# One queue for the stores of gated tiles: SyncE instead of ScalarE, and later in program order

## The chip, the cores and the metric

The kernel runs on one core of a Trainium2 chip. The metric is the device time of one execution in microseconds (us); lower is better. The core has five engines with a queue each: TensorE (PE in the profile, with its weight loads as PEld), VectorE (DVE), ScalarE (ACT), GpSimd (POOL) and SyncE (SP). An engine works through its queue in order. A DMA is begun by an instruction in the queue of SyncE, ScalarE or GpSimd.

## What is computed

The reference mixes two maps of one input `x` (2048 rows, 640 columns) by a gate of each row. Part A is the real part of a Fourier transform over columns and rows, done with matrices. Part B picks, for each row and each of 32 heads, two of 256 experts by product keys, and sums their weighted outputs.

```python
g = sigmoid((x * gate_w).sum(-1, keepdims=True))
# A: y = Cr @ (x @ Dr^T) - Ci @ (x @ Di^T)
a = einsum("bsd,ed->bse", x, dft_hid_re);  b = einsum("bsd,ed->bse", x, dft_hid_im)
y = einsum("ts,bse->bte", dft_seq_re, a) - einsum("ts,bse->bte", dft_seq_im, b)
# B: two best of 16 keys in each half, two best of the four sums, gates, experts
s1 = einsum("nhd,ed->nhe", q1, k1);  s2 = einsum("nhd,ed->nhe", q2, k2)
...
act = gelu(einsum("nd,nhkd->nhk", xf, u[top_e]))
out = einsum("nhk,nhk,nhkd->nd", softmax(top_s), act, v[top_e])
return g * y + (1 - g) * out
```

## The kernel before, in words

**The sequence product.** The kernel turns part A round: it first multiplies the sequence matrices (real and imaginary, 2048 x 2048) with `x`, and later the result with the 640 x 640 hidden matrices. The sequence product runs over 8 columns `q`: two matrices `w` times four blocks `c` of 512 rows (`q = 4 w + c`). Each column is summed over 16 pieces `s` of 128 rows of `x`, so there are 128 pieces `n` in all, `n = 16 q + s`. In one piece, `seq_piece(n)`, TensorE adds to five banks, one for each `d` of five 128-wide parts of the 640 columns. For float32 accuracy each product is three matmuls of high and low parts (`mm3`, L146, L147, L148): high x high, high x low and low x high.

**How a piece is fed.** `load_piece(n + 5)` has SyncE begin the load of a 128 x 512 block of the matrix (`wf<-in_wsre` or `wf<-in_wsim`, L180). `split_piece(n + 3)` makes its high and low parts in one of four slots of `WS`. In most pieces ScalarE rounds the high part (L141) and GpSimd subtracts it (L142). In others, among them the even pieces from 76 to 90, ScalarE makes the high part (L191) and its negative (L192), and GpSimd begins a DMA that adds the block from memory once more onto the negative (L194). The parts `X[s]` of `x` are on the chip only in part: eleven of 16 are stored in `xd` and loaded again by SyncE (L473, `get_x`), in the first half of the product three pieces or more before they are used.

**The gated tiles.** In the last piece of a column ScalarE copies the five banks to five staging tiles `ST` (L249). A row of gates is loaded, VectorE multiplies the five tiles with it (`gate_piece`, L220), and `store_piece` stores them to `pd[w, c]` (L230). Seven columns are stored by ScalarE, the last one by SyncE. The staging tiles come round again in the next column, 16 pieces later. Column 5 stays on the chip too, as `P22`, and is changed in place by later sums (`sum_parts`, L1062).

**The order.** The program is written out in one order, with a table `then`: `at(n, f)` puts a step behind piece `n`, and `follow(n)` runs the steps of piece `n` in the order in which they were put there. Every engine gets its instructions in that order. Between the products of a piece, `run_bg` takes steps of background work from a queue: the picking of experts, and later the building of expert masks (`experts`, L869 on VectorE), which TensorE uses in groups of 128 small matmuls (L883) whose results ScalarE scales (L820) and VectorE adds up (L826). SyncE also does transposing DMAs for the expert rows (L719), and the loads of `draw` (L921), which become the hidden matrices `DD` (split at L141 and L142).

Of the kernel before, what the change touches and what calls it, by code (L numbers as in the profile page):

```python
# [28 lines left out]
NC = S // TC  # L29
NPC = 2 * NC * NT  # L30
KD = D // P
# [78 lines left out]
def gated_mix_kernel(ctx: ExitStack, tc: tile.TileContext, xT, xn, dreT, dimT, wsre, wsim, wq, kT, uT, vv, gw, out):  # L110
    nc = tc.nc
# [38 lines left out]
    pd = {(w, c): dram.tile([KD, P, TC], F32, name=f"pd{w}{c}", tag=f"pd{w}{c}") for w in range(2) for c in range(NC)}  # L150
# [48 lines left out]
    def at(n, f, *args):  # L199
        then.setdefault(n, []).append(lambda: f(*args))  # L200
# [8 lines left out]
    grow, staged, P22 = {}, {}, {}  # L209
# [5 lines left out]
    def gate_piece(q):  # L215
        g = grow.pop(q)
        w, c = divmod(q, NC)
        for d in range(KD):
            f = staged.pop((q, d))
            nc.vector.scalar_tensor_tensor(f, f, -1.0 if w else 1.0, g, op0=OP.mult, op1=OP.mult)  # L220
            bg.credit -= 0.75
            staged[q, d] = f

    def store_piece(q, chunks=range(KD)):
        w, c = divmod(q, NC)
        if q == NC + 1:
            P22.update((d, staged[q, d]) for d in range(KD))
        eng = nc.sync if q == 2 * NC - 1 else nc.scalar
        for d in chunks:
            eng.dma_start(pd[w, c][d], staged.pop((q, d)))  # L230

    def seq_piece(n):
        w, c, s = pieces[n]
# [18 lines left out]
    for q in range(2 * NC):  # L252
        n = NT * (q + 1)
        at(n + (2 if q == 0 else -2 if q > 1 else -1), load_row, q)
        at(n + (7 if q == 0 else 0), gate_piece, q)
        if q in (1, 2, 3, 4):
            for d in range(KD):
                at(n + 1 + d, store_piece, q, (d,))
        else:
            at(n + (12 if q == 0 else 1), store_piece, q)  # L260


    p1_stack = ctx.enter_context(ExitStack())
# [63 lines left out]
    for n in range(WARM):  # L327
        c = slice(0, 2 * P) if n < WARM - 1 else slice(2 * P, TC)
# [172 lines left out]
    n = b + 2  # L501
# [274 lines left out]
    for p in range(NP):  # L776
        n = N0 + 4 * p + min((p + 1) // 2, 3)
# [296 lines left out]
    for k, (n, m) in enumerate(((-1, 2), (0, 4), (5, 7), (7, 9), (10, 12))):  # L1074
        n, m = NT * (NC + 2) + n, NT * (NC + 2) + m
# [255 lines left out]
```

## Time and profile before

| | |
|---|---|
| median of 3 runs | 753.0 us (752.62 to 753.67) |
| the profiled execution's own time | 753.65 us |
| its span, first to last instruction | 751.9 us |
| mean granted TensorE clock | 0.997 |
| busy: TensorE, VectorE, ScalarE, GpSimd | 745.9, 579.0, 337.0, 344.0 us |
| DMA | 171.17 MB, mean 228 GB/s |
| stores `pd<-ST` begun by ScalarE / by SyncE | 35 / 5, of 256 KB each |

The profile is of one execution. A row of a timeline gives the start, the duration, the engine (with q for its queue alone, where it issues or waits), the source line, the operation, and in brackets the idle time ahead of it and what ended that. A row of waits gives the total, the number and the longest. The chain of waits is followed back from the end: at each step to what released the instruction, or to the one before it on its engine. The duration of a DMA in the chain is from its start to its landing.

### The profile page before, as it was taken

The numbers are of one execution on the slowest core, as the hardware profiler recorded it, in microseconds if no ns is written. First come the engines' busy times: TensorE is split into PE (matmuls) and PEld (weight loads), VectorE is DVE, ScalarE is ACT, GpSimd is POOL, SyncE is SP. The second block draws the span as 40 slices with busy tenths as digits, with TensorE's granted clock in tenths as the row PEclk, the third lists the DMA queues.
The fourth block names the chain that finished last, engine by engine and source line by source line (L and its number), as shares of the span: only waits on it lengthen the run. The fifth ranks groups of instructions, "written<-read, shape, count | busy, mean of one in ns | idle before, by whom it ended". The sixth has DMA issues, their size and how long they took to land.

```text
span 751.9 us, 12032 instructions
## 1 busy us (share of the span) xinstructions
PE 745.9 (99%) x4437; PEld 606.4 (81%) x4437; DVE 579.0 (77%) x721; ACT 337.0 (45%) x564; POOL 344.0 (46%) x286
## 2 busy tenths in 40 slices
PE   9999999999999999999999999999999999999998
PEld 7777777888888888888888887888888888888887
DVE  6864087595999899999999959998798874357651
ACT  4335234543545745655454565422344553443451
POOL 5533324540532424235145655544356693487253
PEclk9999999999999999999999999999999999999999
DMA  9999999887656785971498675398855789875302
GB/s 338 372 384 359 331 364 380 232 237 234 140 171 148 195 245 134 254 204 54 134 406 276 150 189 160 95 320 265 285 194 185 227 259 305 258 235 178 112 29 71
DMA packets 84491, 171.17 MB, mean 228 GB/s; under 512 B 16080, under 2 KB 21328, under 8 KB 84176
## 3 DMA queue, kind: packets, MB, share of 16 engines
q1 hardware_dynamic: 70960, 146.13, 57.9%
q0 software_dynamic: 5472, 9.96, 8.4%
q10 hardware_dynamic: 8000, 14.31, 5.2%
q8 instruction: 35, 0.57, 0.3%
q14 instruction: 24, 0.20, 0.1%
HBM read 136.40 MB, written 32.39 MB: 224 GB/s over the span
## 4 chain that ended last, share of the span: by engine, by line
PE 96%; DMA 2%; SPq 1%; ACT 0%; POOL 0%; issue 0%; DVE 0%; ACTq 0%
PE b L146 30%; PE b L147 30%; PE b L148 30%; PE b L383 2%; PE b L242 2%; PE b L883 1%; DMA wf<-in_wsim 1%; DMA WS<-in_wsim 1%; PE b L329 1%; SPq L719 0%; ACT rows L724 0%; POOL DD L142 0%; SPq L921 0%; SPq L180 0%; ACT DD L141 0%
## 5 line engine op out<-in xcount | busy, mean ns | idle before, releaser
L146 PE MATMUL b<-WS,X 128*128 128x512 f32 x620 | 243.8, 393 | 0.0
L147 PE MATMUL b<-WS,X 128*128 128x512 f32 x620 | 241.9, 390 | 1.9 <-DMA WS<-in_wsim 1.9
L148 PE MATMUL b<-WS,X 128*128 128x512 f32 x620 | 241.8, 390 | 0.0
L142 POOL TENSOR_TENSOR WS<-wf,WS 128x512 fp32r<-128x512 f32 x89 | 131.5, 1481 | 177.4 <-ACT WS L141 173.1
L146 PEld LDWEIGHTS b<-WS,X 128*128 128x128 f32 x620 | 116.7, 188 | 28.2 <-issue 4.1
L147 PEld LDWEIGHTS b<-WS,X 128*128 128x128 f32 x620 | 116.8, 188 | 26.0 <-DMA WS<-in_wsim 2.3
L148 PEld LDWEIGHTS b<-WS,X 128*128 128x128 f32 x620 | 116.7, 188 | 24.6
L141 ACT ACTIVATE WS<-wf 128x512 fp32r<-128x512 f32 x89 | 55.5, 627 | 110.5 <-PE b L148 68.3
L869 DVE TENSOR_TENSOR hot<-rows,wtab 128x1024 f16<-128x1024 f16 x56 | 54.1, 1000 | 12.4 <-PE b L883 12.4
L142 POOL TENSOR_TENSOR xl<-xf,xh 128x640 fp32r<-128x640 f32 x16 | 26.8, 1680 | 72.5 <-ACT xh L141 72.5
L570 ACT ACTIVATE sc<-b 128x512 f32<-128x512 f32 x32 | 19.9, 620 | 78.8 <-PE b L148 75.0
L194 POOL DMA_DIRECT2D WS<-in_wsre x30 | 26.3, 878 | 61.0 <-ACT WS L192 59.7
L142 POOL TENSOR_TENSOR WS<-ra,WS 128x512 fp32r<-128x512 f32 x33 | 46.6, 1423 | 15.3 <-ACT WS L141 10.4
L141 ACT ACTIVATE WS<-ra 128x512 fp32r<-128x512 f32 x47 | 29.4, 631 | 42.7 <-PE b L148 30.6
L625 DVE TENSOR_TENSOR eq<-sc,mm 128x1024 f16<-128x1024 f32 x32 | 44.4, 1388 | 0.9
L632 DVE TENSOR_REDUCE tied<-eq 128x64 f32<-128x1024 f16 x32 | 39.0, 1218 | 0.9
L623 DVE TENSOR_REDUCE mm<-sc 128x64 f32<-128x1024 f32 x32 | 38.7, 1210 | 0.2
L220 DVE SCALAR_TENSOR_TENSOR ST<-ST,grow 128x512 f32<-128x512 f32 x40 | 33.9, 902 | 0.6 <-ACT ST L249 0.6
L142 POOL TENSOR_TENSOR WP<-ra,WP 128x512 fp32r<-128x512 f32 x13 | 19.3, 1492 | 31.0 <-ACT WP L141 30.9
L147 PE MATMUL b<-WU,xh 128*128 128x512 f32 x80 | 31.1, 389 | 0.0
L146 PE MATMUL b<-WU,xh 128*128 128x512 f32 x80 | 31.1, 389 | 0.0
L148 PE MATMUL b<-WU,xl 128*128 128x512 f32 x80 | 31.1, 389 | 0.0
(213 smaller groups left out, 1431.0 us busy)
## 6 DMA issues: line engine op xcount, KB each, us to landing
X<-xd SPq DMA_DIRECT2D x36, 640.0 KB, 6.5
wq<-in_wq SPq DMA_DIRECT2D x32, 640.0 KB, 7.5
wf<-in_wsim SPq DMA_DIRECT2D x64, 256.0 KB, 4.9
wf<-in_wsre SPq DMA_DIRECT2D x63, 256.0 KB, 6.6
ra<-pd SPq DMA_DIRECT2D x40, 256.0 KB, 3.4
pd<-ST ACTq DMA_DIRECT2D x35, 256.0 KB, 4.5
WS<-in_wsre POOLq DMA_DIRECT2D x30, 256.0 KB, 6.2
xd<-X SPq DMA_DIRECT2D x11, 640.0 KB, 9.1
```

Of the source, the lines that this page charges most:

```text
L141: nc.scalar.activation(h, f, AF.Copy)
L142: eng.tensor_sub(l, f, h.bitcast(F32))
L146: nc.tensor.matmul(o, wh, ah, start=first, stop=False, skip_group_check=more)
L147: nc.tensor.matmul(o, wh, al, start=False, stop=False, skip_group_check=more)
L148: nc.tensor.matmul(o, wl, ah, start=False, stop=last, skip_group_check=more)
L194: nc.gpsimd.dma_start(l, (wsre, wsim)[w][c, s], accum_op=OP.add)
L220: nc.vector.scalar_tensor_tensor(f, f, -1.0 if w else 1.0, g, op0=OP.mult, op1=OP.mult)
L570: copy = lambda o, f: nc.scalar.activation(o, f, AF.Copy)
L623: nc.vector.tensor_reduce(m, sc, op=OP.max, axis=AX.X)
L625: nc.vector.tensor_tensor(eq, sc, m[:, :, None].to_broadcast([P, HH, E]), op=OP.is_equal)
L632: nc.vector.tensor_reduce(tied[:, s, ib, :], eq, op=OP.add, axis=AX.X)
L869: nc.vector.tensor_tensor(o, a, b, op=op)
```

## The change

All 40 stores of gated tiles are begun by SyncE. The steps lie further on in program order: columns 1 to 4 store one tile behind each of the pieces `n + 3` to `n + 7` instead of `n + 1` to `n + 5` (`n` is the first piece after the column); column 0 stores behind piece `n + 13` instead of `n + 12`; column 6 behind `n + 3` instead of `n + 1`; column 5 stores one tile behind `n + 1`, two behind `n + 2` and two behind `n + 3`, instead of all behind `n + 1`; column 7 stays where it is. `P22` is noted when the tiles are gated, which issues no instruction.

```diff
             bg.credit -= 0.75
             staged[q, d] = f
+        if q == NC + 1:
+            P22.update((d, staged[q, d]) for d in range(KD))
 
     def store_piece(q, chunks=range(KD)):
         w, c = divmod(q, NC)
-        if q == NC + 1:
-            P22.update((d, staged[q, d]) for d in range(KD))
-        eng = nc.sync if q == 2 * NC - 1 else nc.scalar
         for d in chunks:
-            eng.dma_start(pd[w, c][d], staged.pop((q, d)))
+            nc.sync.dma_start(pd[w, c][d], staged.pop((q, d)))
...
         if q in (1, 2, 3, 4):
             for d in range(KD):
-                at(n + 1 + d, store_piece, q, (d,))
+                at(n + 3 + d, store_piece, q, (d,))
+        elif q == NC + 1:
+            for d in range(KD):
+                at(n + 1 + (d + 1) // 2, store_piece, q, (d,))
         else:
-            at(n + (12 if q == 0 else 1), store_piece, q)
+            at(n + (13 if q == 0 else 1 if q == 2 * NC - 1 else 3), store_piece, q)
```

## The prediction

> **What bounds the kernel.** I read the page first, then a table of stretches, TensorE's timeline, the chain of waits, and the timelines of ScalarE, VectorE and SyncE around the one place where TensorE stops.
>
> ```profile
> span 751.9 us, 12032 instructions
> ...
> PE 745.9 (99%) x4437; PEld 606.4 (81%) x4437; DVE 579.0 (77%) x721; ACT 337.0 (45%) x564; POOL 344.0 (46%) x286
> ...
> PE 96%; DMA 2%; SPq 1%; ACT 0%; POOL 0%; issue 0%; DVE 0%; ACTq 0%
> ...
> L147 PE MATMUL b<-WS,X 128*128 128x512 f32 x620 | 241.9, 390 | 1.9 <-DMA WS<-in_wsim 1.9
> ```
>
> TensorE is busy 99% of the span; the chain that ends last is TensorE but for 4%. A gain can come only from an idle stretch of TensorE or from slow matmuls. Among the costliest groups one matmul line has idle time: 1.9 us, ended by an accumulating DMA of GpSimd into a low part (`WS<-in_wsim`, L194). Next the table of that place (us, busy time and count of PE, PEld, DVE, ACT, POOL, granted clock, DMA share, GB/s) and TensorE's timeline.
>
> ```profile
> 453.17:455.42 2.25, 0.38 (x2) 0.00 (x1) 2.23 (x2) 2.25 (x3) 1.91 (x2) 1.00 1.04 310
> 455.42:461.56 6.14, 6.14 (x142) 4.87 (x143) 4.99 (x6) 1.91 (x4) 3.22 (x2) 0.72 0.80 211
> 438.13:442.96 4.83, 4.83 (x144) 3.89 (x143) 2.89 (x4) 3.19 (x4) 1.41 (x2) 1.00 0.87 206
> 449.77:453.17 3.40, 3.40 (x17) 2.81 (x15) 1.35 (x3) 3.33 (x6) 1.40 (x2) 1.00 0.96 241
> ```
> ```profile
> 453.17 0.39 PE L146 MATMUL b<-WS,X 128*128 128x512 f32 x1
> 455.42 0.50 PE L147 MATMUL b<-WS,X 128*128 128x512 f32 x1 [1.87 <-DMA WS<-in_wsim]
> 455.75 0.40 PE L148 MATMUL b<-WS,X 128*128 128x512 f32 x1
> 456.08 1.27 PE L883 MATMUL b<-hot 128*32 128x32 f16 x128
> ...
> 474.58 1.10 PE L883 MATMUL b<-hot 128*32 128x32 f16 x110
> ```
>
> A plain piece of the sequence product takes 3.40 us; one with a group of 128 small expert matmuls (L883) takes 4.83. The piece from 453.17 to 461.56 (piece 88) has such a group and takes 2.25 + 6.14 = 8.39: 3.56 over. Of that 1.87 is the idle time, and 1.69 is slow running: the granted clock is 1.00 in the ordinary pieces and 0.72 in the 6.14 us behind the stop. So this stop costs 3.56 us.
>
> The Trainium skill (*TensorE: Matmul & The Clock Gate*, "HAM oscillation") gives as the abstract rule that idle gaps over about 3.4 us bite. The trace disagrees here, since 1.87 us were enough; by the rule, the stop would be worth 1.87.
>
> Who made it late? The chain of waits backwards, and ScalarE beside it:
>
> ```profile
> 440.35 6.48 DMA wf<-in_wsim
> ...
> 446.90 0.33 ACTq L230
> ...
> 447.28 0.75 ACT DD L141
> ...
> 448.10 1.51 POOL DD L142
> ...
> 449.62 5.76 DMA WS<-in_wsim
> ...
> 455.42 0.50 PE b L147
> ```
> ```profile
> 440.78 1.26 ACT L820 ACTIVATE b<-b,mask_t 128x256 f32<-128x256 f32 x2
> ...
> 447.92 0.62 ACT L191 ACTIVATE WS<-wf 128x512 fp32r<-128x512 f32 x1
> ...
> 450.52 1.26 ACT L820 ACTIVATE b<-b,mask_t 128x256 f32<-128x256 f32 x2
> ```
> ```profile
> 425.88 3.09 DVE L220 SCALAR_TENSOR_TENSOR ST<-ST,grow 128x512 f32<-128x512 f32 x5
> ...
> 451.81 0.69 DVE L826 TENSOR_REDUCE cd<-b 128x256 f32<-128x512 f32 x1 [5.04 <-ACT b L820]
> ...
> 454.72 0.68 DVE L869 TENSOR_TENSOR hot<-hot,rows 128x1024 f16<-128x1024 f16 x1
> 456.57 3.21 DVE L869 TENSOR_TENSOR hot<-rows,wtab 128x1024 f16<-128x1024 f16 x2 [1.17 <-PE b L883]
> ...
> 472.63 0.68 DVE L869 TENSOR_TENSOR rows<-rows,rows 128x1024 f16<-128x1024 f16 x1
> ```
>
> ScalarE ends L820 at 442.04, and its next item is a store of a gated tile (L230), begun at 446.90: a hold of 4.86 us. The tile was ready, since all five gates ended by 428.97. What ended 0.07 us earlier is a load, at 440.35 + 6.48 = 446.83, which the store does not read. So a store waits for the landing of another DMA, begun by SyncE, and holds what stands behind it on ScalarE: the split of `DD`, the high part of piece 88 (L191), and L820, for which VectorE waits 5.04. The same kind of wait shows on SyncE:
>
> ```profile
> SPq L473 <- DMA pd<-ST: 9.0, 2, 5.2
> ```
>
> **The change, part by part.** *35 issues leave ScalarE and join SyncE.*
>
> ```profile
> L230 ACTq DMA_DIRECT2D pd<-ST x35: 326/326/499, 123.3 to 552.3; - x35
> L230 SPq DMA_DIRECT2D pd<-ST x5: 319/384/1859, 600.1 to 603.9; - x5
> ```
>
> 35 x 0.326 = 11.4 us of queue time leave an engine that is 45% busy: nothing by itself. On SyncE 35 x 0.384 = 13.4 us are added, at most five per 16 pieces; the loads behind each move by 0.4 us. Cover: a block of `wf` is begun five pieces ahead, 5 x 3.40 = 17 us.
>
> *The hold at 442.04.* Without the store, ScalarE splits `DD` by about 442.9 and then needs the load of piece 88, the first of the pair that SyncE begins at 439.34:
>
> ```profile
> 439.34 1.50 SPq L180 DMA_DIRECT2D wf<-in_wsim  x2
> ...
> L180 SPq DMA_DIRECT2D wf<-in_wsim x9: 328/402/958, 439.3 to 459.3; - x9
> ...
> DMA to landing us min/median/max: 3.4/5.3/6.6
> ```
>
> By the nine loads of 436 to 462 it lands 3.4 to 6.6 later, at 442.7 to 445.9. I take the late end, since the load behind it took 6.48. In the new order the store of the first tile follows this load instead of preceding it. So L191 starts at 446.0, 1.9 earlier than 447.92, and what follows moves with it: the accumulating DMA starts at 449.62 - 1.9 = 447.7 and lands after 5.76, at 453.5. TensorE wants it at 453.17 + 0.23 (a fifteenth of 3.40) = 453.40: 0.1 us is left. The bounds come from all eight such DMAs:
>
> ```profile
> L194 POOL DMA_DIRECT2D WS<-in_wsim x8: 862/884/903, 401.1 to 454.2; - x8
> ...
> DMA to landing us min/median/max: 4.1/5.5/7.1
> ```
>
> that is 451.8 to 454.8, or 0 to 1.4 left. Next late is the expert group: L820 at 450.52 - 1.9 lets VectorE end its build at 455.40 - 1.9 = 453.5, and TensorE comes to L883 at 453.40 + 2 x 0.23 = 453.86, so it is hidden with 0.36 to spare. Then the following group: VectorE resumes 456.08 - 453.86 = 2.22 earlier, at 454.35, has work for 473.31 - 456.57 = 16.74, and ends at 471.1; TensorE would come there at 453.86 + 18.50 (474.58 - 456.08) - 1.5 of the slow time = 470.9. That leaves 0.2. Sum: -3.56 + 0.1 + 0.2 = -3.3 us.
>
> *The other blocks.* Columns 1 to 3 and 6 wait two pieces longer, column 0 one. Their staging buffers are next written 16 pieces on, and their gates are done when SyncE, which runs ahead of TensorE, comes there. Only for column 5 may it come too early:
>
> ```profile
> 488.80 5.28 DVE L220 SCALAR_TENSOR_TENSOR ST<-ST,grow 128x512 f32<-128x512 f32 x5
> ...
> 487.69 5.60 SPq L180 DMA_DIRECT2D wf<-in_wsim  x4
> ```
>
> The four loads that end at 493.29 now have the five stores between them; the last gate ends at 494.08, so the loads behind move by up to 1.5 us, against 17 us of lead: nothing now. Where such cover is gone, each us of stop costs 3.56 / 1.87 = 1.9 us. The update of `P22` at the gate issues nothing; column 7 stays.
>
> The Trainium skill (*DMA: Bandwidth & Descriptors*, "Issuing engines are not separate DMA queues") says that starting DMAs on several engines saves only the sequencer time of the start, all running on the same 16 DMA engines. The row of 0.33 us per issue agrees; the hold of 4.86 us is what it leaves out.
>
> The profiled execution took 753.65 (span 751.9 and 1.75 around it), so the sum is 750.4; the median is 0.65 lower, and I take half of that off: 750.1.
>
> **Rivals.** *Half of it returns*: the accumulating DMA lands at its slow end (1.4 left), or the load of 88 is later because three stores now begin in the crowded 440 to 448 instead of before. 1.2 us of idle time x 1.9 = 2.3 instead of 0.3: 752.1. For it: DMA shares of 0.87 to 1.04 there. Against it: only one store would be under way before that load's successor.
>
> *Only the clock's part stays out*: if the slow running is not tied to so short a stop, the idle time alone is saved: 753.0 - 1.87 = 751.1. The 0.72 speaks against it, a single occurrence for it.
>
> *Only issue time moves*: ScalarE waits for the same load anyway, in L191: 753.0. The landing bounds of 442.7 to 445.9 speak against it. The skill's rule on issuing engines gives this outcome.
>
> *Slower: SyncE's one queue delays the X loads.* Column 3's stores now stand between the loads of `X`, in a stretch that has nothing to spare:
>
> ```profile
> 372.00:400.00 28.00, 28.00 (x125) 23.21 (x124) 27.52 (x27) 13.73 (x15) 12.22 (x9) 1.00 0.97 369
> ...
> L473 SPq DMA_DIRECT2D X<-xd x9: 319/432/1113, 372.7 to 399.0; - x9
> ...
> DMA to landing us min/median/max: 4.6/8.2/9.2
> ```
>
> A load of `X` is asked for three pieces ahead, 10.2 us; the slowest takes 9.2, so it decides once a load lands over 1.0 later. A store of 262,144 bytes at 369 GB/s is 0.71; five in a row 3.6, less 1.0 is 2.6 of stop, x 1.9 = 4.9: 750.1 + 4.9 = 755.0. Against it: the same bytes share the same DMA engines today, and TensorE loses nothing in these 28 us.
>
> **How the numbers follow.** About 0.2% (1.5 us) is what a measurement of this kernel tells from none, so faster means below 751.5, slower above 754.5. The forecast has 0.58, all faster. Half returned: 0.17 (0.07 faster, 0.10 same). Clock: 0.07 (0.05 and 0.02). Issue time only: 0.08, same. X loads: 0.10, slower. Together 0.70, 0.20, 0.10. The low end is 753.0 - 3.56 = 749.4, less 0.2 for half of the distance to the fastest run (752.62); the high end is the whole 1.4 left, 753.0 - 3.56 + 1.4 x 1.9 + 0.2 = 752.3, and twice that 0.2: 752.7. That leaves out the slower case and nearly all of issue time only.
>
> **What would show it.** Right: no L230 on ScalarE; L820 and L191 of piece 88 about 2 us nearer to the work before them; piece 88 at 4.8 to 5.3 us at clock 1.00; all other pieces at 3.40 or 4.83. Wrong: TensorE idle before L147 again (half returned), before L146 behind an `X` or `wf` load (SyncE's queue), or before L883 (VectorE is the bound).

## The result

Before: 753.34 us (median of 6 runs, 752.62 to 754.61). After: 750.24 (6 runs, 749.20 to 750.59). The ratio is 0.9956, 95% interval 0.9943 to 0.9969. The profiled execution took 750.55 of its own time. Nearly all of the gain lies at one piece of TensorE's work. Two runs of those told below lay far outside the others (1067.52 for all stores early, 2569.01 for the kernel before) and stand in no median, range or count here.

From the page of the kernel after, with the queue of ScalarE's and SyncE's DMAs (packets, MB, share of the DMA engines; q10, of ScalarE, had 8000 packets before and q1, of SyncE, 70960), the chain by engine, and two of the costliest groups:

```profile
span 748.7 us, 12034 instructions
...
PE 744.1 (99%) x4437; PEld 605.1 (81%) x4437; DVE 577.2 (77%) x721; ACT 336.8 (45%) x564; POOL 344.3 (46%) x286
...
q1 hardware_dynamic: 76000, 155.31, 60.7%
...
q10 hardware_dynamic: 2960, 5.13, 1.9%
...
PE 95%; DMA 3%; DVE 1%; POOL 0%; SPq 0%; ACT 0%; issue 0%
...
L147 PE MATMUL b<-WS,X 128*128 128x512 f32 x620 | 241.3, 389 | 0.0
...
L146 PE MATMUL b<-WU,xh 128*128 128x512 f32 x80 | 31.2, 390 | 0.5 <-ACT b L572 0.5
```

The idle time of 1.9 us before L147 is gone. Another has come, 0.5 us before L146 in the product of `x` with the query weights (`WU,xh`), far from any store. Line numbers have moved: L230 is now L229 and L249 is L248, and behind the changed places they are two higher (L820 is L822, L883 is L885).

The table of stretches, first piece 88 of the kernel after and the stretch around the new stop, then that stretch before the change:

```profile
453.56:458.39 4.83, 4.83 (x145) 3.89 (x143) 3.58 (x3) 1.87 (x4) 3.23 (x2) 1.00 1.04 299
135.39:142.96 7.57, 7.09 (x31) 5.55 (x30) 7.32 (x8) 3.79 (x9) 6.45 (x7) 1.00 0.45 101
```
```profile
135.85:142.70 6.85, 6.85 (x31) 5.60 (x30) 6.54 (x8) 3.41 (x7) 5.66 (x6) 1.00 0.49 100
```

Piece 88 takes 4.83 us at clock 1.00, not 8.39: 3.56 less. It starts 0.39 later than before (453.56, not 453.17): TensorE came to the early stretch 0.46 earlier, lost 7.57 - 6.85 = 0.72 in it, and 0.13 more on the way to piece 88 (310.60 us from 142.96, where it had been 310.47 from 142.70). So 0.39 - 3.56 = -3.17, and the span is 3.2 shorter (751.9 to 748.7). Nothing else of size happens.

The timelines of the kernel after around piece 88, one for each engine: TensorE, ScalarE, GpSimd, VectorE, SyncE.

```profile
139.43 0.50 PE L146 MATMUL b<-WU,xh 128*128 128x512 f32 x1 [0.48 <-ACT b L572]
...
453.56 0.39 PE L146 MATMUL b<-WS,X 128*128 128x512 f32 x1
453.78 0.39 PE L147 MATMUL b<-WS,X 128*128 128x512 f32 x1
...
471.40 0.78 PE L885 MATMUL b<-hot 128*32 128x32 f16 x75
```
```profile
441.91 0.73 ACT L141 ACTIVATE DD<-draw 128x640 fp32r<-128x640 f32 x1
444.72 0.64 ACT L191 ACTIVATE WS<-wf 128x512 fp32r<-128x512 f32 x1 [2.08 <-DMA wf<-in_wsim]
...
447.36 1.25 ACT L822 ACTIVATE b<-b,mask_t 128x256 f32<-128x256 f32 x2
```
```profile
446.43 0.88 POOL L194 DMA_DIRECT2D WS<-in_wsim  x1 [1.88 <-ACT WS L192]
```
```profile
448.64 0.69 DVE L828 TENSOR_REDUCE cd<-b 128x256 f32<-128x512 f32 x1 [0.53 <-ACT b L822]
```
```profile
439.40 0.42 SPq L180 DMA_DIRECT2D wf<-in_wsim  x1
439.93 0.44 SPq L229 DMA_DIRECT2D pd<-ST  x1
440.41 0.43 SPq L180 DMA_DIRECT2D wf<-in_wsim  x1
```

ScalarE splits `DD` as soon as L822 is done (441.91) and then waits only for the load of block 88, which it needs. L191 starts 3.20 us earlier than before (447.92), L822 3.16 earlier (450.52), and VectorE waits 0.53 where it waited 5.04.

### The profile page after: what moved, and what is told of

Its sections match the earlier page's. It is cut to its first block, busy times and chain, and to the rows that moved or that the text cites. A ratio compares the mean times of both kernels' runs of the same rounds, so it can differ in the third digit from the quotient of the medians.

```text
span 748.7 us, 12034 instructions
## 1 busy us (share of the span) xinstructions
PE 744.1 (99%) x4437; PEld 605.1 (81%) x4437; DVE 577.2 (77%) x721; ACT 336.8 (45%) x564; POOL 344.3 (46%) x286
## 4 chain that ended last, share of the span: by engine, by line
PE 95%; DMA 3%; DVE 1%; POOL 0%; SPq 0%; ACT 0%; issue 0%
PE b L146 30%; PE b L147 30%; PE b L148 30%; PE b L385 2%; PE b L241 2%; PE b L885 1%; DMA xd<-X 1%; DMA wf<-in_wsre 1%; DMA X<-xd 1%; PE b L331 1%; POOL xl L142 0%; DVE xf L458 0%; DVE xf L459 0%; SPq L376 0%; DVE xf L461 0%; DVE xf L460 0%
## 5 line engine op out<-in xcount | busy, mean ns | idle before, releaser
L146 PE MATMUL b<-WS,X 128*128 128x512 f32 x620 | 243.1, 392 | 0.0
L147 PE MATMUL b<-WS,X 128*128 128x512 f32 x620 | 241.3, 389 | 0.0
L146 PEld LDWEIGHTS b<-WS,X 128*128 128x128 f32 x620 | 116.4, 188 | 28.2 <-issue 4.1
L147 PEld LDWEIGHTS b<-WS,X 128*128 128x128 f32 x620 | 116.4, 188 | 23.6
L871 DVE TENSOR_TENSOR hot<-rows,wtab 128x1024 f16<-128x1024 f16 x56 | 50.6, 939 | 15.3 <-PE b L885 15.3
L146 PE MATMUL b<-WU,xh 128*128 128x512 f32 x80 | 31.2, 390 | 0.5 <-ACT b L572 0.5
L147 PE MATMUL b<-WU,xh 128*128 128x512 f32 x80 | 31.1, 389 | 0.0
```

Source lines behind the costliest of these rows:

```text
L146: nc.tensor.matmul(o, wh, ah, start=first, stop=False, skip_group_check=more)
L147: nc.tensor.matmul(o, wh, al, start=False, stop=False, skip_group_check=more)
L871: nc.vector.tensor_tensor(o, a, b, op=op)
```

## The experiments

The runs came on three chips, each with runs of the kernel before beside them: its medians there were 753.90 (34 runs), 754.01 (20) and 753.02 (22). The ratios are against the kernel before on the same chip. The kernel after was run only for the result, so that comparisons with it go across chips.

**Only column 4 is changed**, in the kernel before:

```diff
-        eng = nc.sync if q == 2 * NC - 1 else nc.scalar
+        eng = nc.sync if q in (NC, 2 * NC - 1) else nc.scalar
...
-                at(n + 1 + d, store_piece, q, (d,))
+                at(n + (3 if q == NC else 1) + d, store_piece, q, (d,))
```

> Before, with column 4's five stores alone begun by SyncE, behind pieces 83 to 87. Theory A (the gain is the removal of one hold of ScalarE, ahead of piece 88): the whole gain, 750.2 (749.6 to 751.0), piece 88 at 4.8 us and no idle time before its L147. Rival B (ScalarE gains from every one of the 35 issues): a seventh of the 3.1 us, 752.9. Rival C (the other columns on SyncE cost or give something of their own): more than 0.7 us away from the changed kernel.

Measured: 750.47 (749.11 to 751.95, 11 runs), ratio 0.9957 (0.9942 to 0.9973). Its profile still has a stop of 0.58 us before L147 of piece 88, where none was expected. **Everything but column 4** in the kernel after:

```diff
-            nc.sync.dma_start(pd[w, c][d], staged.pop((q, d)))
+            (nc.scalar if q == NC else nc.sync).dma_start(pd[w, c][d], staged.pop((q, d)))
...
-                at(n + 3 + d, store_piece, q, (d,))
+                at(n + (1 if q == NC else 3) + d, store_piece, q, (d,))
```

> The changed kernel, with column 4's five stores back on ScalarE, behind pieces 81 to 85. Theory A: the hold is back, its store again begun at the landing of the load of block 89; idle time of 1 to 2.5 us before L147 of piece 88, 753.3 (752.5 to 754.3). Rival B: six sevenths of the gain stay, 750.7. Rival C: away from the kernel before by over 0.7 us.

Measured: 754.38 (751.67 to 756.11, 12 runs), ratio 1.0003 (0.9986 to 1.0020). The whole gain is column 4; the other six columns are worth nothing that this resolves. The chain of waits of this second kernel shows the hold again:

```profile
439.62 6.34 DMA wf<-in_wsim
...
446.04 0.33 ACTq L229
...
446.41 0.75 ACT DD L141
...
448.74 6.77 DMA WS<-in_wsim
...
455.56 0.50 PE b L147
```

The load lands at 439.62 + 6.34 = 445.96; 0.08 later ScalarE's store begins.

**What the store waits for.** A completion semaphore is a counter that a DMA raises when its data has landed. The trace records which one each DMA raises: the 519 DMAs of SyncE and ScalarE, apart from those of GpSimd, take the same eight in turn, in program order. A DMA waits until the one eight places ahead has landed, and its engine's queue stands while it waits: in the trace of the kernel before, all of the 511 pairs that share a semaphore in this way keep to it. The order around the fourth store of column 4, numbered as in the program before the change:

```text
295 SyncE   load of block 88       298-300     transposing DMAs of SyncE
296 SyncE   load of block 89       301-303     loads of blocks 90 to 92
297 ScalarE third store            304 ScalarE fourth store: waits for 296
```

If that is so, one more small DMA between 297 and 304 makes the fourth store wait for 297 instead. In the kernel before, SyncE loads 16 KB into a tile that nothing reads:

```diff
+    kt2 = const.tile([P, 2, E], F32)
+    at(84, lambda: nc.sync.dma_start(kt2, kT))
```

> The kernel before, all stores as they were, with one more DMA: SyncE loads the 16 KB of key columns a second time, behind piece 84, into a tile that nothing reads. Theory A': a store waits for the DMA that is eight places ahead of it in the program's order of the DMAs of SyncE and ScalarE. With one more in between, the fourth store of column 4 waits for the third store (landed at 442.9 before) and no longer for the load of block 89 (446.8). So the hold ends about 4 us earlier and, although work is only added, the time falls to 750.4 (749.6 to 751.5). Rival F (the store waits for DMA bandwidth or for ScalarE's own queue of DMAs): no gain, 753.9 or more.

Measured: 750.40 (749.50 to 753.22, 7 runs), ratio 0.9949 (0.9930 to 0.9967). ScalarE's queue in its timeline (third and fourth store), and the landing of the third from the answer for that line:

```profile
438.63 0.33 ACTq L230 DMA_DIRECT2D pd<-ST  x1
...
443.38 0.35 ACTq L230 DMA_DIRECT2D pd<-ST  x1
```
```profile
DMA to landing us min/median/max: 4.7/4.7/4.7
```

The third store lands at 438.63 + 4.7 = 443.3, and the fourth begins at 443.38, 3.52 earlier than in the kernel before. The load of block 89 landed no sooner: begun at 439.81, it took at least 6.7, to 446.5, and the fourth store no longer waited for it. Work was only added, and the gain is that of the whole change. Neither the engine nor the position of the store is needed for it.

**The last two stores of column 4 one piece later**, still by ScalarE, in the kernel before:

```diff
-                at(n + 1 + d, store_piece, q, (d,))
+                at(n + 1 + d + (q == NC and d > 2), store_piece, q, (d,))
```

> The kernel before, with the fourth and fifth store of column 4 one piece later (behind 85 and 86), still begun by ScalarE. Theory A': both now stand behind the split of piece 88 in ScalarE's queue and wait for transposes that are older than the load of block 89; the stop before piece 88 goes: 750.4 (749.6 to 751.5). Rival G (only moving off ScalarE helps): 753.9.

Measured: 751.09 (750.68 to 752.38, 7 runs), ratio 0.9961 (0.9945 to 0.9977). The stop is gone here too; the first L147 of piece 88 has no idle time ahead of it:

```profile
454.13 0.39 PE L147 MATMUL b<-WS,X 128*128 128x512 f32 x1
```

By the trace, the two stores now share their semaphores with two of the transposing DMAs, and ScalarE begins them at 450.12 and 450.62, behind the split of piece 88.

**The new places, ScalarE's engine**: the kernel after with

```diff
-            nc.sync.dma_start(pd[w, c][d], staged.pop((q, d)))
+            (nc.sync if q == 2 * NC - 1 else nc.scalar).dma_start(pd[w, c][d], staged.pop((q, d)))
```

> The later places in program order of the change, but the seven columns' stores still begun by ScalarE. Theory A, by the order of the DMAs in the program: the second store of column 4 now stands behind piece 84, where the fourth stood, and the DMA that it has to wait for is again the load of block 89; so the hold stays, ends at about 446.9, and the time is 753.3 (752.3 to 754.3). Rival D (the later place is what helps, since ScalarE then finds older DMAs landed): 750.2.

Measured: 753.54 (752.36 to 756.58, 12 runs), ratio 1.0008 (0.9991 to 1.0024). Its timeline, of ScalarE's queue and of TensorE:

```profile
446.27 0.33 ACTq L229 DMA_DIRECT2D pd<-ST  x1
```
```profile
456.19 0.50 PE L147 MATMUL b<-WS,X 128*128 128x512 f32 x1 [2.37 <-DMA WS<-in_wsim]
```

Two pieces later means that the second store has come to the fourth's old place, held by the same load (begun at 439.7, landed 6.5 later). So "later" is no remedy as such; which DMA is eight places ahead decides.

**SyncE's engine, the old places**, in the kernel after:

```diff
-                at(n + 3 + d, store_piece, q, (d,))
-        elif q == NC + 1:
-            for d in range(KD):
-                at(n + 1 + (d + 1) // 2, store_piece, q, (d,))
+                at(n + 1 + d, store_piece, q, (d,))
         else:
-            at(n + (13 if q == 0 else 1 if q == 2 * NC - 1 else 3), store_piece, q)
+            at(n + (12 if q == 0 else 1), store_piece, q)
```

> All stores begun by SyncE, but at their old places in program order. Theory A: ScalarE is freed as in the change; SyncE waits for gates instead, longest for column 6 (the gates run 547 to 552, SyncE is there about 540) and column 5, about 12 and 6 us, which the five pieces of lead cover: 750.4 (749.6 to 751.2). Rival E (the later places are needed, since the waiting stores hold the loads): idle time of TensorE before L146 or L147 behind a load, 1 us of stop or more, 752 to 756.

Measured: 751.34 (750.50 to 753.97, 11 runs), ratio 0.9968 (0.9952 to 0.9983): between the ranges of the two theories, so that neither is right as it stands. Its profile, the slowest of these runs, has two stops in TensorE's timeline, and slow running in the stretch behind the second:

```profile
382.49 0.47 PE L146 MATMUL b<-WS,X 128*128 128x512 f32 x1 [0.39 <-DMA X<-xd]
...
455.92 0.50 PE L147 MATMUL b<-WS,X 128*128 128x512 f32 x1 [1.80 <-DMA WS<-in_wsim]
```
```profile
455.92:461.64 5.72, 5.72 (x142) 4.49 (x143) 4.45 (x6) 4.91 (x7) 2.67 (x2) 0.70 1.00 317
```

No store holds ScalarE here. L191 of piece 88 waits for its own load, which SyncE begins at 440.76, behind one more store than in the kernel after, where it begins at 439.40:

```profile
447.55 0.63 ACT L191 ACTIVATE WS<-wf 128x512 fp32r<-128x512 f32 x1 [4.70 <-DMA wf<-in_wsim]
```

**Only column 3 early**, and **only column 4 early**, in the kernel after, take this apart:

```diff
-                at(n + 3 + d, store_piece, q, (d,))
+                at(n + (1 if q == 3 else 3) + d, store_piece, q, (d,))     # or q == 4
```

> The changed kernel, with column 3's stores on SyncE but at their old places, behind pieces 65 to 69. If SyncE's wait for the gate of column 3 is what the old places cost: the X load of piece 68 starts about 5 us later, TensorE stops before it (0.4 us as in the run with all old places) or at piece 76, and the time is 750.2 to 751.4, 0.3 to 1.0 above the changed kernel. If it is column 4 alone: as the changed kernel.

> The changed kernel, with column 4's stores on SyncE but at their old places, behind pieces 81 to 85. If column 4 is what the old places cost: three stores stand ahead of the load of block 88 or beside it, which lands at about 447.4 instead of 444.6; a stop of 1 to 2 us before L147 of piece 88 and 751.0 to 752.5. If it is column 3 alone: as the changed kernel, 750.4.

Measured: column 3 early 751.77 (751.37 to 752.59, 12 runs), ratio 0.9975 (0.9962 to 0.9988); column 4 early 751.00 (750.03 to 752.90, 7 runs), 0.9959 (0.9943 to 0.9975). On the same chip the small load had 750.40 and the later pair 751.09; column 3 early came out somewhat above the range expected of it. With column 3 early, SyncE's queue, its waits in that stretch, and TensorE:

```profile
373.76 0.32 SPq L229 DMA_DIRECT2D pd<-ST  x1
...
377.93 0.52 SPq L475 DMA_DIRECT2D X<-xd  x1
```
```profile
SPq L229 <- DVE ST L220: 4.8, 1, 4.8
```
```profile
382.63 0.47 PE L146 MATMUL b<-WS,X 128*128 128x512 f32 x1 [0.29 <-DMA X<-xd]
```

SyncE runs ahead of TensorE, comes to the first store before its gate is done, and waits 4.8 us; the load of `X` behind it begins at 377.93, where the kernel after begins it at 372.99:

```profile
372.99 0.52 SPq L475 DMA_DIRECT2D X<-xd  x1
```

That costs a stop of 0.29 and leaves the next three loads of `X` 0.1 to 0.8 us to spare; there is one more stop, of 0.49, before the expert group at 423.40, and no run shows whether it belongs to the early stores. In the kernel after the same wait is 0.2 us. So the places further on do have a use with SyncE: they keep its queue clear of the gates of column 3. Column 4 early has no effect that these runs resolve, and its profile has no stop before L147 of piece 88.

**The stop put back by other means.** In the kernel after, ScalarE makes the high part of piece 88 four times, or seven times, instead of once:

```diff
-            nc.scalar.activation(h, f, AF.Copy)
+            for _ in range(4 if n == 88 else 1):
+                nc.scalar.activation(h, f, AF.Copy)
```

> The changed kernel, with the high part of piece 88 made four times over by ScalarE (same values), which holds what follows by 3 x 0.65 = 2.0 us. If the hold of ScalarE is what counts, whoever causes it: the stop before L147 of piece 88 comes back with 0.4 to 1.7 us. Clock: if the drop follows from the length of the stop (0.72 behind 1.87 us in the kernel before), piece 88 takes 4.83 + the stop + about 1.5, 752 to 753.5 in every run; if it hangs on where the stop falls in a window of the clock's own, some runs have it and some do not, as the runs with 2.4 us and clock 1.00 had it not: 751 to 752.2, with a wide spread.

> The same with seven times over, 6 x 0.65 = 3.9 us of hold: a stop of 2.4 to 3.6 us. By the length of the stop, 4 to 5.2 us over the changed kernel, 754.4 to 755.6, and clock under 1 in the piece behind it. By a window: 752.8 to 755.6, by run.

Measured: four times 753.20 (750.25 to 756.00, 10 runs), ratio 0.9996 (0.9981 to 1.0012); seven times 755.98 (753.45 to 756.85, 10 runs), 1.0026 (1.0012 to 1.0039). The stretches up to and behind the stop: four times, then seven times, then for comparison the stretch behind the stop in the kernel with everything but column 4:

```profile
453.99:455.86 1.87, 0.39 (x2) 0.00 (x0) 0.45 (x1) 1.43 (x3) 0.99 (x2) 1.00 1.03 347
455.86:460.59 4.73, 4.73 (x142) 3.81 (x143) 3.58 (x5) 0.90 (x2) 1.91 (x2) 1.00 0.97 287
```
```profile
453.86:457.59 3.73, 0.38 (x2) 0.00 (x1) 2.31 (x3) 3.28 (x4) 2.88 (x3) 1.00 1.01 288
457.59:463.28 5.69, 5.69 (x142) 4.47 (x143) 4.36 (x7) 0.90 (x2) 1.90 (x2) 0.70 0.57 149
```
```profile
455.56:460.28 4.72, 4.72 (x143) 3.80 (x143) 3.58 (x5) 0.90 (x2) 2.36 (x2) 1.00 0.77 197
```

The mean granted clock of the stretch was 0.70 behind a stop of 3.35 us, and 1.00 behind 1.49 and 2.46, and behind the 2.37 of the new places on ScalarE. It was 0.72 behind 1.87 in the profile of before, and 0.70 behind 1.80 with all stores early. So a stop of about 2 us sometimes brings slow running and sometimes not; the expectations by length alone and by a window each met only a part of this.

The clock records of the traces say more. Each drop behind a stop is to 0.50 and lasts 3.413 us, and in all 13 profiles every change of the clock lies a whole number of steps of 3.413 us behind the start of that profile's record: 132 steps in the kernel before, from 6.39 to 456.95. Here are the steps around the stop in the kernel before, with four times the high part, and with everything but column 4:

```profile
453.54:456.95 3.41, 1.54 (x107) 1.17 (x107) 2.24 (x3) 2.98 (x5) 2.48 (x3) 1.00 0.92 278
456.95:460.36 3.41, 3.41 (x50) 2.77 (x40) 3.41 (x4) 0.81 (x2) 2.28 (x2) 0.50 0.91 214
```
```profile
453.56:456.97 3.41, 1.92 (x65) 1.09 (x64) 0.88 (x2) 1.86 (x3) 2.53 (x3) 1.00 0.97 316
456.97:460.38 3.41, 3.41 (x103) 2.89 (x92) 3.37 (x5) 0.90 (x2) 0.80 (x1) 1.00 1.03 304
```
```profile
450.88:454.29 3.41, 2.22 (x10) 1.50 (x8) 3.34 (x4) 3.38 (x6) 2.60 (x2) 1.00 1.03 276
454.29:457.70 3.41, 2.15 (x131) 1.74 (x132) 1.24 (x2) 1.94 (x5) 2.56 (x2) 1.00 0.88 240
457.70:461.12 3.42, 3.42 (x16) 2.79 (x16) 3.42 (x6) 0.87 (x3) 0.22 (x1) 1.00 0.62 168
```

TensorE's idle time within one step was 3.41 - 1.54 = 1.87 in the kernel before, 1.80 with all stores early and 3.01 with seven times the high part; the next step ran at 0.50. With four times it was 1.49, and the stops of 2.46 and 2.37 are cut in two by the end of a step, with at most 1.26 and 1.36 in one; there the clock stayed. So in these six profiles it is not the length of the stop that decides but how much of it falls into one step, and the limit lies between 1.49 and 1.80 us. No run was made to test this.

**The margin of the accumulating DMA.** In the kernel after, GpSimd subtracts the low parts of pieces 78 and 88 instead of beginning a DMA for them:

```diff
-            if not N0 + 4 <= n < (4 * NT if n % 2 else ACCUM_END) or 4 * NT <= n < N1 + 10:
+            if not N0 + 4 <= n < (4 * NT if n % 2 else ACCUM_END) or 4 * NT <= n < N1 + 10 or n in (78, 88):
```

> The changed kernel, with the low parts of pieces 78 and 88 subtracted by GpSimd (1.4 us) and no longer added by a DMA of 4 to 8 us. These two had the least time to spare (0.7 and 0.3 us in the changed kernel's profile, stops of 0.2 and 0.6 in two of the others). If such small stops are part of the changed kernel's usual time: 749.9 (749.3 to 750.4), 0.3 to 0.6 below it; if they are rare: the same, 750.3.

Measured: 750.97 (750.41 to 751.62, 6 runs), ratio 0.9963 (0.9950 to 0.9976): no gain over the kernel after, and above what either outcome was to give. So no version here is shown to beat the changed kernel; the small load's 750.40 lies within the range of the changed kernel's runs.

**What the runs' clocks say.** Each run has its mean granted clock. One drop takes 0.5 x 3.413 / 752 = 0.002 off it. Of 76 runs of the kernel before, 36 had 0.999 or 1.000, with a median of 752.5; 31 had 0.997 or 0.998, median 754.4; nine had 0.995 or 0.996, median 756.1. Of 56 runs of the seven kernels without a long stop at piece 88 (after, column 4 alone, small load, one piece later, either column early, two by GpSimd), none was below 0.999. With four times the high part, six runs at 0.999 or above had a median of 752.3 and four below 754.4.

## Why the prediction was right

It gave 750.1 with 749.2 to 752.7, from 753.0 before; measured 750.24, from 753.34. That is a gain of 3.1 where 2.9 was forecast.

**Who bounds, and the price of the stop.** Right. A loss of 3.56 us at piece 88 went to nothing. **The cause** is shown: a store that waited for the landing of a load which it does not read, and held ScalarE. The prediction could not say why it waited; the place eight DMAs ahead explains it, and the small load, which leaves engine and place of every store and shifts only which DMAs are paired from there on, moved the time from 754.0 to 750.4.

**The sum.** In the profile of the kernel after, the pieces differ from the forecast, and that their errors cancel is luck. The load of block 88 landed at 439.40 + 5.2 = 444.6 rather than the late end 446.0, so L191 began at 444.72 and the accumulating DMA at 446.43, not 447.7. That DMA took 7.07 instead of 5.76 and landed at 453.50. TensorE wanted it at 453.78, since it came 0.39 later: 0.28 to spare, where 0.1 of stop was forecast. In the profiles of four other kernels without the hold (column 4 alone, small load, one piece later, column 4 early) L191 waited for that load until 446.2 to 446.8, near the forecast, and the accumulating DMA took 5.4 to 6.9; two of them have a stop there, of 0.58 and 0.22. So the forecast of next to nothing to spare is borne out. The following expert group, forecast 0.2 late, came without idle time at 471.40. In their place stands the new stop of 0.48 at 139.43. It is 0 in the profile before; among the other kernels it is between 0 and 1.24, and 1.24 is that of column 4 alone, which leaves all that is written ahead of piece 80 as before. So it is not tied to the change; what sets it was not found.

**The mis-sized term** is the slow running. The prediction took 1.69 us of it as part of this stop, at 1.9 us for each us of idle time. It comes with this stop only in about half the runs. Beside the idle time, about 0.28 goes with any such stop (piece 88 ran 1.77 over with 1.49 of stop, 2.74 over with 2.46), and the slow running adds 5.69 - 4.73 = 0.96 to 6.14 - 4.73 = 1.41 in a piece when it comes. By the medians of the runs, an estimate across chips, a stop of 2 us is worth some 2.3 in a run that keeps its clock (752.5 - 750.2) and 4.2 in one of 0.997 or 0.998 (754.4 - 750.2); that the two differ by 1.9, more than the 0.96 to 1.41 of the profiles, stays open. The profiled run before was one of the latter (0.997), so the sum, made against its time, came out close. On the chip with the most runs, moving column 4 alone is worth 753.9 - 750.5 = 3.4, a mean over both kinds.

**The rivals.** *Half of it returns*: no; column 4 alone had 0.58 of stop in its profile and still a median of 750.47, so a part of it can come back in single runs. *Only the clock's part stays out*: it was right on one thing, that so short a stop does not always bring slow running, and wrong on the time, since before pays for it in half its runs. *Only issue time moves*: no. ScalarE does then wait for a load in L191, as this rival said, but for that of block 88, and in these five profiles L191 began 1.1 to 3.2 us earlier than the 447.92 of the kernel before. *SyncE's one queue delays the X loads*: its mechanism exists, not in this change but with the old place of column 3, and there by waiting for a gate rather than by the bytes of the stores. A load begun 4.9 us later cost 0.29 in one stop, and the time was 0.7 to 1.4 above the two good kernels on that chip, where the prediction had a cost of 4.9.

**Column 5** cost nothing, as argued. These two rows of SyncE's queue in the kernel after are its first and last stores there:

```profile
487.61 0.32 SPq L229 DMA_DIRECT2D pd<-ST  x1
...
490.82 0.90 SPq L229 DMA_DIRECT2D pd<-ST  x2
```

## What to carry to other kernels

When an instruction that issues a DMA stands for microseconds though its data is ready, look at what landed just before it began: it may be waiting for an earlier, unrelated DMA whose semaphore it takes over, and everything behind it on that engine waits too. Count the DMAs between the two; one DMA more or less, or the issue on an engine with nothing urgent behind it, moves the wait, and a move "later" may only put another DMA into the same place. Price a stop by several runs and their clocks, not by the one that was profiled: what it costs can depend on where it falls.

## What was unexpected of the hardware

The clock fell to half for 3.413 us behind stops of 1.80 and 1.87 us and did not behind 2.37 and 2.46. The Trainium skill (*TensorE: Matmul & The Clock Gate*, "What's actually happening") describes a free-running activity window of about 3.4 us, and says that the point at which the clock rises depends on where in it the first matmul lands. The traces agree with such a window, and show its like for a stop: the changes lie on steps of 3.413 us, and 40 of 76 runs of the kernel before were below 0.999. They do not agree with the 3.4 us that the page ("HAM oscillation") gives as the bound for idle gaps: 1.80 us within one step were enough.

One load of 16 KB that nothing reads made the kernel 3.6 us faster. And the Trainium skill (*DMA: Bandwidth & Descriptors*, "Issuing engines are not separate DMA queues") counts only the sequencer's time as saved by issuing on another engine: here that is 0.33 us for one store, while the choice of the engine decided who stood for the 4.86 us of its wait.
